# Turning q, k and y by one transposing DMA per block instead of on TensorE, in a gated linear attention and feed-forward kernel

## The chip, the cores and the metric

The kernel runs on one core of a Trainium2 chip. The metric is the device time of one execution in microseconds. Engines are named as in the profile: PE is TensorE's matrix multiply, PEld its weight loads, DVE is VectorE, ACT is ScalarE, POOL is GpSimd, and SP is SyncE, which here does nothing but issue DMAs. "SPq" and "ACTq" are DMAs issued by SP and by ACT.

## The reference

A gated linear attention over 4 batches, 8 heads, 768 steps and a head size of 48 is followed by a feed-forward layer with 384 inputs, 2048 hidden units, and the activation s * relu(h)^2 + b.

```
for t in range(S):
    state = alpha[:, :, t, :, None] * state + np.einsum('bhd,bhe->bhde', k[:, :, t], v[:, :, t])
    y[:, :, t] = np.einsum('bhd,bhde->bhe', q[:, :, t], state)
x = y.transpose(0, 2, 1, 3).reshape(B * S, H * D)
h = x @ w_in
r = np.maximum(h, 0.0)
g = s * (r * r) + b
out = g @ w_out
```

Inputs and output are float32; the kernel multiplies in bfloat16.

## The kernel before

The 3072 rows are worked through in 24 blocks of 128 steps, six to a batch. In one block the attention is computed in its chunked form, with all 8 heads beside each other (48 columns each, in pairs of heads):

- `ln` takes the logarithm of alpha on ACT, `cum` sums it over the block by a matmul with a triangular matrix, and ACT gives the cumulative decay `b_sb` and its inverse `bi_sb`. `decay` brings the block's last row of `b_sb` to the layout of `blast`: one DMA to DRAM (`row_dr`) and two back from there, all issued by SP.
- `qk` scales q and k on DVE (`qb_sb`, `kb_sb`, with time on the partitions). `vcast` casts v on POOL.
- `tr` turns scaled q and k on PE, eight transposes by an identity (L244) into `ct_ps`, and DVE copies them to `qkT_sb` (L249), with the head's columns on the partitions.
- `amat` multiplies k by q per head into `a_ps` and masks the result on DVE.
- `y` (that is, `yp` and `st`) gives the block's output in `y_ps` from `am` and v and from the state `sd_sb` of the block before, and the new state by PE, DVE (`t1_sb`) and POOL (`sd_sb`, `sc_sb`). ACT copies `y_ps` to `y_bf` (L305).
- `xt` turns `y_bf` on PE by three transposes into `h_ps` (L312), and ACT copies them to `xd_sb` (L318), the input of the feed-forward layer.
- `m`, four times a block (u = 0 to 3), multiplies `xd_sb` by a quarter of w_in (twelve matmuls, L365), takes relu on ACT (`r_sb`, L379) and squares it on DVE (`gt_sb`, L386). This is what "products" means in this document. `o`, four times a block, multiplies `gt_sb` by a quarter of w_out (L402). After the fourth, blocks 0 to 12 are kept in SBUF by an ACT copy (`keep_sb`, in the space of the w_in staging), since the bias row isn't known yet; the later ones get the bias added on DVE (L415) and go out through `store` (L438). The kept blocks get theirs by `add_bias` (L441), one every 5.5 positions from position 117.3 on, each with a `store` of its own.

Inputs are loaded per block by four DMAs on SP (`load`: alpha, k, q, v, 192 KB each, in rows of 192 bytes), five blocks ahead, into rings of eight buffers. Other rings have two or three buffers. Two PSUM banks `h_ps` serve the products in turn, with `xt` between them.

Each engine runs its instructions in the order in which the program issues them. That order is written out by hand: `at(position, function, ...)` puts a piece of work at a position, and at the end all pieces are called in order of position. Block n has its `y` at p = 8n, so eight positions are one block. For a block in the steady part, `cum` stands at p - 14.8, `qk` right behind, `tr` at p - 10.8, `amat` at p - 7.9, `y` at p, `xt` at p + 1, `m` at p + 2.5 to p + 7.5, `o` at p + 8.5 to p + 14.5. SP's queue is ordered by the same positions: what stands in it behind a waiting DMA waits too. A DMA's completion is counted on one of eight semaphores, which are used in turn.

Of the kernel before, what the change touches and what calls it, by code (L numbers as in the profile page):

```python
# [9 lines left out]
BF16 = mybir.dt.bfloat16  # L10
# [4 lines left out]
def kernel(  # L15
# [12 lines left out]
    nc = tc.nc  # L28
# [34 lines left out]
    def ring(name, shape, dtype, n):  # L63
        return [sb.tile(shape, dtype, name=f"{name}{i}") for i in range(n)]
# [33 lines left out]
    for g, sz in enumerate(GROUPS):  # L98
        first_block.append(sum(GROUPS[:g]))
        u0 = first_block[g] % UNITS  # L100
        xd_sb.append(xd_all[:, u0 : u0 + sz].rearrange("a u x -> a (u x)").rearrange("a (t s) -> a t s", t=KT))
# [106 lines left out]
    def cum(n):  # L208
        la = la_sb[n % 2]
        nc.tensor.matmul(out=cum_ps, lhsT=U_bf, rhs=la[:, :, 0:48], start=True, stop=True)  # L210
# [12 lines left out]
        if n < NCH - 1:  # L223
            nc.scalar.activation(out=blast[n % 3][0:112, :, 0], in_=tot_ps[0:112], func=AF.Exp)
        elif n % NCH < NCH - 1:
            decay(n)

    def decay(n):
        row = row_dr[n % 3]
        nc.sync.dma_start(out=row, in_=b_sb[n % 2].rearrange("s h d -> s (h d)")[127:128])  # L230
        for e in range(2):
            nc.sync.dma_start(
                out=blast[n % 3][64 * e : 64 * e + 48, :, 0],
                in_=row.rearrange("o (p e d) -> e d (o p)", e=2, d=48)[e],
            )

    def qk(n):
        nc.vector.tensor_tensor(out=kb_sb[n % 3][:, :, 0:48], in0=k_sb[n % NLD], in1=bi_sb[n % 2], op=ALU.mult)  # L238
        nc.vector.tensor_tensor(out=qb_sb[n % 2][:, :, 0:48], in0=q_sb[n % NLD], in1=b_sb[n % 2], op=ALU.mult)  # L239

    def tr(n):
        for x, t in ((0, qb_sb[n % 2]), (1, kb_sb[n % 3])):
            for p in range(NP):
                nc.tensor.transpose(  # L244
                    out=t_ps[0:112, x, p, :],
                    in_=t.rearrange("a h d -> a (h d)")[:, 128 * p : 128 * p + 112],
                    identity=ident,
                )
        nc.vector.tensor_copy(  # L249
            out=qkT_sb[n % 2][0:112].rearrange("a x p t -> a (x p t)"),  # L250
            in_=t_ps[0:112].rearrange("a x p t -> a (x p t)"),
        )

    def amat(n):
        qkT = qkT_sb[n % 2]
        for p in range(NP):
            for e in range(2):
                r0 = 64 * e
                nc.tensor.matmul(  # L259
                    out=a_ps[e][:, p, :],  # L260
                    lhsT=qkT[r0 : r0 + 48, 1, p, :],
                    rhs=qkT[r0 : r0 + 48, 0, p, :],
                    start=True,
                    stop=True,
                )
        for e in range(2):
            nc.vector.tensor_tensor(out=am_sb[e][n % 2], in0=a_ps[e], in1=mask4, op=ALU.mult)  # L267
# [6 lines left out]
    def yp(n):  # L274
        c = n % NCH
        if c > 0:
            for p in range(NP):
                nc.tensor.matmul(  # L278
                    out=y_ps[:, 96 * p : 96 * p + 96],
                    lhsT=qkT_sb[n % 2][0:112, 0, p, :],  # L280
                    rhs=sd_sb[(n - 1) % 2][0:112, p, :],
                    start=(p == 0),
                    stop=False,
                    skip_group_check=True,
                )
        for h in range(H):
            nc.tensor.matmul(  # L287
                out=y_ps[:, 48 * h : 48 * h + 48],
                lhsT=am_sb[h % 2][n % 2][:, h // 2, :],
                rhs=v_bf[n % 3][:, h, :],  # L290
                start=(c == 0 and h == 0),
                stop=(h == H - 1),
                skip_group_check=True,
            )
        if c < NCH - 1:
            kb = kb_sb[n % 3].rearrange("a h d -> a (h d)")
            for p in range(NP):
                nc.tensor.matmul(
                    out=pst[:, p, :],
                    lhsT=kb[:, 128 * p : 128 * p + 128],  # L300
                    rhs=v_bf[n % 3][:, 2 * p : 2 * p + 2, :],
                    start=True,
                    stop=True,
                )
        nc.scalar.activation(out=y_bf[n % 2], in_=y_ps[:, 0 : H * 48], func=AF.Copy)  # L305


    def xt(n):
        hp = h_ps[nrelu[0] % 2].bitcast(BF16)[:, 0 : KT * C]
        nrelu[0] += 1  # L310
        for kk in range(KT):
            nc.tensor.transpose(  # L312
                out=hp[:, kk * C : (kk + 1) * C],
                in_=y_bf[n % 2][:, 128 * kk : 128 * (kk + 1)],
                identity=ident,
            )
        g, i = group_of[n]
        nc.scalar.activation(  # L318
            out=xd_sb[g][:, :, i * C : (i + 1) * C],
            in_=hp.rearrange("a (t s) -> a t s", t=KT),  # L320
            func=AF.Copy,
        )
# [71 lines left out]
    def mm2(g, t, u):  # L394
        if g == NBLK - 1:
            return last(u)
        N = GROUPS[g] * C
        op = o_ps
        if g in o_in_a:
            op = a_ps[o_in_a[g]].rearrange("a p t -> a (p t)")  # L400
        for j in range(4 * u, 4 * u + 4):
            nc.tensor.matmul(  # L402
                out=op[:, 0:d_model],
                lhsT=gt_sb[g][:, j * N + t * C : j * N + (t + 1) * C],
                rhs=w_out_bf[:, j, :],
                start=(j == 0),
                stop=(j == NJ - 1),
            )
        if u == 3:
            if g < NKEEP:  # L410
                nc.scalar.activation(out=keep_sb[g], in_=op[:, 0:d_model], func=AF.Copy)
                return
            ot = out_sb[nout[0] % 3]
            nout[0] += 1
            nc.vector.tensor_tensor(out=ot, in0=op[:, 0:d_model], in1=bias_w, op=ALU.add)  # L415
            store(g, ot)


    def last(u):
# [43 lines left out]
    for t in la_sb:  # L463
        nc.vector.memset(t, 0.0)
    nc.vector.memset(ones_c, 1.0)
    for t in qb_sb + kb_sb + blast:
        nc.vector.memset(t, 0.0)
    make_identity(nc, ident)
    for i in range(NP):
# [64 lines left out]
        at(111.5 + 2 * i, bias_row, i)  # L534
    for n in range(NKEEP):
        at(117.3 + 5.5 * n, add_bias, n)
        at(118.2 + 5.5 * n, store, n, keep_sb[n])
    for u in range(1, 4):
        at((30.5, 31.2, 32.5)[u - 1], o, 3, u)
    at(20.0, load, NLD)  # L540
    for n in range(4, NBLK):
        p = 8 * n
        if n > 4:
# [8 lines left out]
        at(p, y, n)  # L552
        if n + 5 < NBLK:
# [37 lines left out]
```

## Time and profile before

| | before |
|---|---|
| median of 3 runs | 199.65 us (199.53 to 199.88) |
| the profiled execution's span, from the first to the last instruction | 198.2 us |
| PE busy | 185.2 us (93%) |
| DVE busy | 150.8 us (76%) |
| ACT busy | 118.8 us (60%) |
| POOL busy | 64.2 us (32%) |
| moved by DMA | 30.33 MB, 113454 packets |

Durations in this document come from one profiled execution. Its span is 1.45 us shorter than the median of the runs; what lies between is before the first instruction and after the last. In the chain of waits each piece is put down to the instruction that ended last; a group of pipelined matmuls counts there with what it adds, which is less than the sum of its instructions' durations.

### The profile page before, as it was taken

Reading aid. Unit: us, or ns where it says so; the run is one execution under the profiler, and the core shown is the slowest. Engines: PE = TensorE matmul, PEld = TensorE weight load, DVE = VectorE, ACT = ScalarE, POOL = GpSimd, SP = SyncE. Lnnn points to the kernel's source line nnn. Section 1 sums busy time; section 2 is a strip of 40 time slices with the busy share of each in tenths; the row PEclk is TensorE's granted clock in tenths of the full one; section 3 lists DMA queues with packets and bytes.
Section 4 is the critical chain, followed back from the end, with each engine's and each line's share of the span. In section 5 each row is a group of like instructions: output and inputs, shape, how many; then the busy total and the mean of one; then the engine's idle time right before and its main releaser. Section 6 shows DMA issues by size and latency. Waiting matters only on the chain.

```text
span 198.2 us, 6120 instructions
## 1 busy us (share of the span) xinstructions
PE 185.2 (93%) x2440; PEld 145.3 (73%) x2440; DVE 150.8 (76%) x296; ACT 118.8 (60%) x243; POOL 64.2 (32%) x96
## 2 busy tenths in 40 slices
PE   1999899988899999999999999999999999999994
PEld 1566587754577688888878877878888877877783
DVE  5467777867466779789877996989987999998532
ACT  3245668381675765766766677666575665664650
POOL 5142251611120136326500633623700851652000
PEclk9999999999999999999999999999999999999999
DMA  7999999999999384693968846958947953122212
GB/s 125 189 342 232 314 283 369 199 177 193 187 172 195 60 142 86 101 159 64 195 84 148 134 68 120 159 93 193 229 87 164 161 176 112 41 82 81 87 37 79
DMA packets 113454, 30.33 MB, mean 153 GB/s; under 512 B 106627, under 2 KB 111890, under 8 KB 113426
## 3 DMA queue, kind: packets, MB, share of 16 engines
q1 hardware_dynamic: 109262, 29.15, 73.7%
q10 hardware_dynamic: 4164, 0.79, 2.8%
q8 instruction: 19, 0.31, 0.7%
q14 instruction: 9, 0.07, 0.1%
HBM read 25.19 MB, written 4.74 MB: 151 GB/s over the span
## 4 chain that ended last, share of the span: by engine, by line
PE 68%; SPq 15%; DMA 10%; DVE 3%; ACT 1%; issue 1%; ACTq 0%; DVEq 0%
PE h_ps L365 25%; PE o_ps L402 25%; DMA q_sb<-in_q_dram 8%; SPq L128 5%; PE ct_ps L244 5%; SPq L147 4%; PE a_ps L259 3%; SPq L125 3%; SPq L122 2%; PE ct_ps L210 2%; PE y_ps L287 2%; PE h_ps L312 2%; DMA al_sb<-in_alpha_dram 2%; SPq L131 1%; PE a_ps L425 1%; PE y_ps L278 1%
## 5 line engine op out<-in xcount | busy, mean ns | idle before, releaser
L379 ACT ACTIVATE r_sb<-h_ps 128x512 bf16<-128x512 f32 x94 | 55.8, 597 | 39.2 <-PE h_ps L365 37.6
L365 PE MATMUL h_ps<-xd_all,w_in_bf 128*128 128x128 bf16 x1128 | 74.8, 219 | 1.5 <-ACT r_sb L379 1.1
L365 PEld LDWEIGHTS <-w_in_bf 128*128 128x128 bf16 x1152 | 69.3, 98 | 8.4 <-issue 2.3
L402 PE MATMUL o_ps<-w_out_bf,gt_all 128*128 128x384 bf16 x336 | 68.5, 326 | 1.4 <-DVE w_out_bf L160 0.7
L386 DVE TENSOR_TENSOR gt_all<-r_sb 128x512 bf16<-128x512 bf16 x96 | 45.3, 484 | 26.5 <-ACT r_sb L379 25.8
L339 POOL TENSOR_TENSOR sd_sb<-t_sb,blast 48x192 bf16<-48x192 f32 x40 | 22.5, 563 | 103.5 <-DVE t_sb L334 67.3
L402 PEld LDWEIGHTS <-gt_all 128*128 128x128 bf16 x368 | 32.5, 98 | 17.4 <-issue 1.8
L343 POOL TENSOR_TENSOR sc_sb<-t_sb,blast 112x384 f32<-112x384 f32 x16 | 21.8, 1362 | 1.3
L206 POOL CAST v_bf<-v_sb 128x384 bf16<-128x384 f32 x24 | 17.7, 744 | 12.9 <-DMA v_sb<-in_v_dram 12.7
L318 ACT ACTIVATE xd_all<-h_ps 128x384 bf16<-128x384 bf16 x24 | 11.8, 490 | 15.5 <-PE h_ps L312 15.5
L249 DVE COPY qkT<-ct_ps 112x1024 bf16<-112x1024 bf16 x24 | 16.4, 685 | 4.8 <-PE ct_ps L244 4.7
L238 DVE TENSOR_TENSOR kb_sb<-k_sb,bi_sb 128x384 bf16<-128x384 f32 x24 | 13.7, 569 | 8.3 <-ACT bi_sb L221 8.2
L267 DVE TENSOR_TENSOR am_a<-a_ps,mask 128x512 bf16<-128x512 f32 x24 | 16.4, 683 | 3.1 <-PE a_ps L259 3.1
L239 DVE TENSOR_TENSOR qb_sb<-q_sb,b_sb 128x384 bf16<-128x384 f32 x24 | 16.7, 694 | 0.0
L267 DVE TENSOR_TENSOR am_b<-a_ps,mask 128x512 bf16<-128x512 f32 x24 | 16.3, 681 | 0.0
L221 ACT ACTIVATE bi_sb<-ct_ps 128x384 f32<-128x384 f32 x24 | 11.7, 487 | 5.2 <-PE ct_ps L213 3.9
L305 ACT ACTIVATE y_bf<-y_ps 128x384 bf16<-128x384 f32 x24 | 11.7, 488 | 4.9 <-PE y_ps L287 4.8
L203 ACT ACTIVATE la_sb<-al_sb 128x384 bf16<-128x384 f32 x24 | 12.4, 516 | 3.6 <-DMA al_sb<-in_alpha_dram 3.6
L210 PE MATMUL ct_ps<-la_sb,U_bf 128*128 128x384 bf16 x24 | 8.2, 340 | 4.6 <-ACT la_sb L203 4.6
L222 ACT ACTIVATE b_sb<-ct_ps 128x384 f32<-128x384 f32 x24 | 11.9, 494 | 0.0
L244 PEld LDWEIGHTS <-qb_sb 128*112 128x112 bf16 x96 | 8.5, 136 | 4.4 <-DVE qb_sb L239 3.2
L259 PE MATMUL a_ps<-qkT 48*128 48x128 bf16 x192 | 10.2, 226 | 1.0 <-DVE qkT L249 0.4
(66 smaller groups left out, 195.0 us busy)
## 6 DMA issues: line engine op xcount, KB each, us to landing
al_sb<-in_alpha_dram SPq DMA_DIRECT2D x24, 192.0 KB, 3.2
k_sb<-in_k_dram SPq DMA_DIRECT2D x24, 192.0 KB, 3.6
q_sb<-in_q_dram SPq DMA_DIRECT2D x22, 192.0 KB, 4.7
v_sb<-in_v_dram SPq DMA_DIRECT2D x22, 192.0 KB, 4.9
w_in_st<-in_moe_w_in_dram SPq DMA_DIRECT2D x4, 768.0 KB
w_out_st<-in_moe_w_out_dram SPq DMA_DIRECT2D x4, 768.0 KB
out_dram<-w_in_st SPq DMA_DIRECT2D x13, 192.0 KB, 2.6
out_dram<-out_sb SPq DMA_DIRECT2D x10, 192.0 KB, 3.4
```

What stands on the lines that cost most here:

```text
L206: nc.gpsimd.tensor_copy(out=v_bf[n % 3], in_=v_sb[n % NLD])
L239: nc.vector.tensor_tensor(out=qb_sb[n % 2][:, :, 0:48], in0=q_sb[n % NLD], in1=b_sb[n % 2], op=ALU.mult)
L244: nc.tensor.transpose(out=t_ps[0:112, x, p, :], in_=t.rearrange("a h d -> a (h d)")[:, 128 * p : 128 * p + 112], identity=ident,)
L249: nc.vector.tensor_copy(out=qkT_sb[n % 2][0:112].rearrange("a x p t -> a (x p t)"), in_=t_ps[0:112].rearrange("a x p t -> a (x p t)"),)
L259: nc.tensor.matmul(out=a_ps[e][:, p, :], lhsT=qkT[r0 : r0 + 48, 1, p, :], rhs=qkT[r0 : r0 + 48, 0, p, :], start=True, stop=True,)
L267: nc.vector.tensor_tensor(out=am_sb[e][n % 2], in0=a_ps[e], in1=mask4, op=ALU.mult)
L339: nc.gpsimd.tensor_tensor(out=sd[r, :, d], in0=t1_sb[r, :, d], in1=bl[r].to_broadcast([48, NP, 48]), op=ALU.mult)
L343: nc.gpsimd.tensor_tensor(out=sc_sb[0:112], in0=t1_sb[0:112], in1=bl[0:112].to_broadcast([112, NP, 96]), op=ALU.mult)
L365: nc.tensor.matmul(out=hp[:, jj * N : (jj + 1) * N], lhsT=w_in_bf[:, kk, 128 * j : 128 * (j + 1)], rhs=xd_sb[g][:, kk, 0:N], start=(kk == ...
L379: nc.scalar.activation(out=rs, in_=h_of.pop((g, u)), func=AF.Relu)
L386: nc.vector.tensor_tensor(out=gt_sb[g][:, u * 512 : (u + 1) * 512], in0=rs, in1=rs, op=ALU.mult)
L402: nc.tensor.matmul(out=op[:, 0:d_model], lhsT=gt_sb[g][:, j * N + t * C : j * N + (t + 1) * C], rhs=w_out_bf[:, j, :], start=(j == 0), sto ...
```

## The change

From block 6 on (`TURN = 6`), up to block 21, `xt` is no longer called, and from block 8 on `tr` neither. In their place `turn(n)` issues one transposing DMA on SP. Its source is a new tile of 128 x 1408 bfloat16 with scaled q and k of block n + 2 (1024 columns) and y of block n (384 columns) side by side; its destination is a tile of 128 x 11 x 128 that holds the eight turned squares of q and k and the three of y. The places that read `qkT_sb` and `xd_sb` read views of it. Both tiles are rings of three.

```diff
+    TURN = 6
-    qb_sb = ring("qb_sb", [128, H, 64], BF16, 2)
-    kb_sb = ring("kb_sb", [128, H, 64], BF16, 3)
+    QK = 2 * H * 64
+    rows_sb = ring("rows_sb", [128, QK + H * 48], BF16, 3)
+    qk_sb = [t[:, 0:QK] for t in rows_sb]
...
-    y_bf = ring("y_bf", [128, H * 48], BF16, 2)
-    qkT_sb = ring("qkT", [128, 2, NP, 128], BF16, 2)
+    cols_sb = ring("cols_sb", [128, 2 * NP + KT, 128], BF16, 3)
+    qkT_sb = [t[:, 0 : 2 * NP].rearrange("a (x p) t -> a x p t", x=2) for t in cols_sb]
...
+        if TURN <= g < NBLK - 2:
+            xd_sb.append(cols_sb[(g + 2) % 3][:, 2 * NP :])
...
+    def turn(n):
+        nc.sync.dma_start_transpose(out=cols_sb[(n + 2) % 3], in_=rows_sb[(n + 2) % 3])
...
-        nc.scalar.activation(out=y_bf[n % 2], in_=y_ps[:, 0 : H * 48], func=AF.Copy)
+        nc.scalar.activation(out=rows_sb[(n + 2) % 3][:, QK:], in_=y_ps[:, 0 : H * 48], func=AF.Copy)
```

For q and k of block n + 2 to be there in time, `ln`, `vcast`, `cum` and `qk` move to p - 19 from block 8 on, and `amat` to p - 6. The row of `decay` is sent to DRAM in `cum`, and its two DMAs back stand six positions later. `turn(n)` stands at p + 0.5 and the loads behind it at p + 0.6. Products and outputs stand up to five positions later (two for block 6, three for 7, four for 8, five from block 9, and less again in the last two blocks).

```diff
         elif n % NCH < NCH - 1:
-            decay(n)
+            nc.sync.dma_start(out=row_dr[n % 3], in_=b_sb[n % 2].rearrange("s h d -> s (h d)")[127:128])
...
+            if n >= TURN + 2:
+                c = 19.0
...
-            at(p - t, tr, n)
-            at(p - a, amat, n)
+            if n < TURN + 2:
+                at(p - t, tr, n)
+                at(p - a, amat, n)
+                at(p - c + 0.3, decay, n)
+            else:
+                at(p - 6.0, amat, n)
+                at(p - 13.0, decay, n)
         at(p, y, n)
+        if turned:
+            at(p + 0.5, turn, n)
+        else:
+            at(p + 1.0, xt, n)
         if n + 5 < NBLK:
-            at(p - 4.0, load, n + NLD - 3)
+            at(p + 0.6 if turned else p - 4.0, load, n + NLD - 3)
+        late = min(max(n - 4, 0), 5.0) if n < NBLK - 2 else (NBLK - 1 - n) * 3.5
         for u in range(4):
-            at(p + (2.5, 3.5, 5.5, 7.5)[u], m, n, u)
-            at(p + (8.5, 9.5, 12.5, 14.5)[u], o, n, u)
-        at(p + 1.0, xt, n)
+            at(p + late + (2.5, 3.5, 5.5, 7.5)[u], m, n, u)
+            at(p + late + (8.5, 9.5, 12.5, 14.5)[u], o, n, u)
+        if NKEEP <= n < NBLK - 1:
+            at(p + late + 16.2, store, n)
```

All stores but the last block's are issued by ACT instead of SP: those of the kept blocks two positions behind their `add_bias` (before 0.9), those of the later blocks 1.7 positions behind their last `o` (before at once).

```diff
-    def store(n, o):
-        nc.sync.dma_start(out=out[n * C : (n + 1) * C, :], in_=o)
+    finished = {n: keep_sb[n] for n in range(NKEEP)}
+
+    def store(n):
+        nc.scalar.dma_start(out=out[n * C : (n + 1) * C, :], in_=finished.pop(n))
```

More of the change, by code (lines that the diff above doesn't have):

```diff
@@ L81 @@
     bi_sb = ring("bi_sb", [128, H, 48], FP32, 2)
-    qb_sb = ring("qb_sb", [128, H, 64], BF16, 2)
-    kb_sb = ring("kb_sb", [128, H, 64], BF16, 3)
+    QK = 2 * H * 64
+    rows_sb = ring("rows_sb", [128, QK + H * 48], BF16, 3)
+    qk_sb = [t[:, 0:QK] for t in rows_sb]
+    qb_sb = [t.rearrange("a (x h d) -> a x h d", x=2, h=H)[:, 0] for t in qk_sb]
+    kb_sb = [t.rearrange("a (x h d) -> a x h d", x=2, h=H)[:, 1] for t in qk_sb]
     v_bf = ring("v_bf", [128, H, 48], BF16, 3)
-    y_bf = ring("y_bf", [128, H * 48], BF16, 2)
-    qkT_sb = ring("qkT", [128, 2, NP, 128], BF16, 2)
+    cols_sb = ring("cols_sb", [128, 2 * NP + KT, 128], BF16, 3)
+    qkT_sb = [t[:, 0 : 2 * NP].rearrange("a (x p) t -> a x p t", x=2) for t in cols_sb]
     am_sb = [ring("am_a", [128, NP, 128], BF16, 2), ring("am_b", [128, NP, 128], BF16, 2)]
@@ L100 @@
         u0 = first_block[g] % UNITS
-        xd_sb.append(xd_all[:, u0 : u0 + sz].rearrange("a u x -> a (u x)").rearrange("a (t s) -> a t s", t=KT))
+        if TURN <= g < NBLK - 2:
+            xd_sb.append(cols_sb[(g + 2) % 3][:, 2 * NP :])
+        else:
+            xd_sb.append(xd_all[:, u0 : u0 + sz].rearrange("a u x -> a (u x)").rearrange("a (t s) -> a t s", t=KT))
         gt_sb.append(gt_all[:, u0 : u0 + sz].rearrange("a u x -> a (u x)"))
@@ L225, in cum @@
         elif n % NCH < NCH - 1:
-            decay(n)
+            nc.sync.dma_start(out=row_dr[n % 3], in_=b_sb[n % 2].rearrange("s h d -> s (h d)")[127:128])
     def decay(n):
         row = row_dr[n % 3]
-        nc.sync.dma_start(out=row, in_=b_sb[n % 2].rearrange("s h d -> s (h d)")[127:128])
+        if n < NCH - 1 or n % NCH == NCH - 1:
+            return
         for e in range(2):
@@ L238, in qk @@
         nc.vector.tensor_tensor(out=kb_sb[n % 3][:, :, 0:48], in0=k_sb[n % NLD], in1=bi_sb[n % 2], op=ALU.mult)
-        nc.vector.tensor_tensor(out=qb_sb[n % 2][:, :, 0:48], in0=q_sb[n % NLD], in1=b_sb[n % 2], op=ALU.mult)
+        nc.vector.tensor_tensor(out=qb_sb[n % 3][:, :, 0:48], in0=q_sb[n % NLD], in1=b_sb[n % 2], op=ALU.mult)
+    def turn(n):
+        nc.sync.dma_start_transpose(out=cols_sb[(n + 2) % 3], in_=rows_sb[(n + 2) % 3])
     def tr(n):
-        for x, t in ((0, qb_sb[n % 2]), (1, kb_sb[n % 3])):
+        for x, t in ((0, qb_sb[n % 3]), (1, kb_sb[n % 3])):
             for p in range(NP):
@@ L249, in tr @@
         nc.vector.tensor_copy(
-            out=qkT_sb[n % 2][0:112].rearrange("a x p t -> a (x p t)"),
+            out=qkT_sb[n % 3][0:112].rearrange("a x p t -> a (x p t)"),
             in_=t_ps[0:112].rearrange("a x p t -> a (x p t)"),
@@ L254, in amat @@
     def amat(n):
-        qkT = qkT_sb[n % 2]
+        qkT = qkT_sb[n % 3]
         for p in range(NP):
@@ L279, in yp @@
                     out=y_ps[:, 96 * p : 96 * p + 96],
-                    lhsT=qkT_sb[n % 2][0:112, 0, p, :],
+                    lhsT=qkT_sb[n % 3][0:112, 0, p, :],
                     rhs=sd_sb[(n - 1) % 2][0:112, p, :],
@@ L313, in xt @@
                 out=hp[:, kk * C : (kk + 1) * C],
[L314 removed]
+                in_=rows_sb[(n + 2) % 3][:, QK:][:, 128 * kk : 128 * (kk + 1)],
                 identity=ident,
@@ L415, in mm2 @@
             nc.vector.tensor_tensor(out=ot, in0=op[:, 0:d_model], in1=bias_w, op=ALU.add)
-            store(g, ot)
+            finished[g] = ot
     def last(u):
@@ L465 @@
     nc.vector.memset(ones_c, 1.0)
-    for t in qb_sb + kb_sb + blast:
+    for t in qk_sb + blast:
         nc.vector.memset(t, 0.0)
@@ L536 @@
         at(117.3 + 5.5 * n, add_bias, n)
-        at(118.2 + 5.5 * n, store, n, keep_sb[n])
+        at(119.3 + 5.5 * n, store, n)
     for u in range(1, 4):
@@ L542 @@
         p = 8 * n
+        turned = TURN <= n < NBLK - 2
         if n > 4:
@@ L549 @@
             at(p - c + 0.2, qk, n)
-            at(p - t, tr, n)
-            at(p - a, amat, n)
+            if n < TURN + 2:
[5 more added lines that the diff above has]
+                at(p - 13.0, decay, n)
         at(p, y, n)
+        if turned:
+            at(p + 0.5, turn, n)
+        else:
+            at(p + 1.0, xt, n)
         if n + 5 < NBLK:
-            at(p - 4.0, load, n + NLD - 3)
+            at(p + 0.6 if turned else p - 4.0, load, n + NLD - 3)
+        late = min(max(n - 4, 0), 5.0) if n < NBLK - 2 else (NBLK - 1 - n) * 3.5
         for u in range(4):
-            at(p + (2.5, 3.5, 5.5, 7.5)[u], m, n, u)
-            at(p + (8.5, 9.5, 12.5, 14.5)[u], o, n, u)
-        at(p + 1.0, xt, n)
+            at(p + late + (2.5, 3.5, 5.5, 7.5)[u], m, n, u)
+            at(p + late + (8.5, 9.5, 12.5, 14.5)[u], o, n, u)
+        if NKEEP <= n < NBLK - 1:
+            at(p + late + 16.2, store, n)
     for _, _, fn, args in sorted(events, key=lambda e: e[:2]):
```

## The prediction

> **What bounds the kernel now.** I read the busy time by stage first, then the chain of waits inside one stage, then the groups of the instructions that the change removes, then the DMA issues and SP's queue. All times are from one profiled execution with a span of 198.2 us; the median of the runs is 199.65 us, so 1.45 us lie outside the span, and I add them at the end. Three stages of one block each, from the view of busy time by window (PE, PEld, DVE, ACT and POOL busy, TensorE clock, DMA share, GB/s):
>
> ```profile
> 74.38:81.42 7.04, 7.04 (x101) 5.79 (x102) 5.53 (x11) 4.81 (x11) 3.23 (x4) 1.00 0.74 121
> 81.42:88.46 7.04, 7.04 (x101) 5.79 (x102) 6.24 (x12) 4.81 (x11) 3.22 (x4) 1.00 0.71 114
> ```
>
> PE is busy all of the 7.04 us of a block, at the full clock; DVE has 0.8 us left, ACT 2.2 us. The chain of waits through the next block (start, length, what) confirms it: every piece is PE.
>
> ```profile
> 88.46 0.76 PE o_ps L402 x4
> 89.21 0.17 PE h_ps L312 x3
> 89.38 0.16 PE ct_ps L210
> ...
> 91.53 0.65 PE o_ps L402 x4
> 92.18 0.45 PE ct_ps L244 x8
> 92.63 0.67 PE h_ps L365 x12
> ...
> 95.17 0.33 PE a_ps L259 x8
> ```
>
> Here a group costs what it adds to the chain, not the duration of its instructions: eight transposes of q and k 0.45 us, three of y 0.17 us, a group of twelve h_ps matmuls 0.67, four o_ps matmuls 0.65. From block 6 (66 us) to the end the kernel is this chain, so PE time saved there is time saved. Before 58 us the chain runs through loads and nothing of the change acts there.
>
> ```profile
> L318 ACT ACTIVATE xd_all<-h_ps 128x384 bf16<-128x384 bf16 x24 | 11.8, 490 | 15.5 <-PE h_ps L312 15.5
> L249 DVE COPY qkT<-ct_ps 112x1024 bf16<-112x1024 bf16 x24 | 16.4, 685 | 4.8 <-PE ct_ps L244 4.7
> ```
>
> These two copies (0.49 us ACT, 0.69 us DVE per block) go with the transposes; both engines have room, so they are worth nothing by themselves. The DMA issues (KB, us from issue to landing) and SP's queue in one block:
>
> ```profile
> al_sb<-in_alpha_dram SPq DMA_DIRECT2D x24, 192.0 KB, 3.2
> ...
> v_sb<-in_v_dram SPq DMA_DIRECT2D x22, 192.0 KB, 4.9
> ...
> blast<-row_dr SPq DMA_DIRECT2D x30, 0.8 KB, 1.9
> ```
>
> ```profile
> 82.62 0.90 SPq L232 DMA_DIRECT2D blast<-row_dr  x2
> 83.58 0.44 SPq L122 DMA_DIRECT2D al_sb<-in_alpha_dram  x1
> 84.11 0.53 SPq L128 DMA_DIRECT2D k_sb<-in_k_dram  x1
> 84.73 0.81 SPq L125 DMA_DIRECT2D q_sb<-in_q_dram  x1
> 85.60 0.72 SPq L131 DMA_DIRECT2D v_sb<-in_v_dram  x1
> 86.42 0.58 SPq L230 DMA_DIRECT2D row_dr<-b_sb  x1
> 89.59 1.81 SPq L232 DMA_DIRECT2D blast<-row_dr  x2
> ```
>
> SP issues for about 4.1 us a block (0.90 + 0.44 + 0.53 + 0.81 + 0.72 + 0.58, and gaps), and stands still from 87.0 to 89.6 because L232 waits for the row of L230. The DMA engines are taken for 0.55 to 0.74 of a block.
>
> **The change part by part.** *Removed from PE:* for 16 blocks (8 to 23) the q and k transposes, 16 x 0.45 = 7.2 us; for 16 blocks (6 to 21) those of y, 16 x 0.17 = 2.7 us. Both lie on the chain: -9.9 us. A block falls from 7.04 to 6.42 us.
>
> *Added: 16 transposing DMAs on SP.* Each moves 128 x 1408 x 2 bytes = 352 KB as 1408 rows of 256 bytes. The trace holds no such DMA. Its landing time, l, is bounded below by the smallest DMA (1.9 us), and by the nearest rows of size it lies between 1.9 + (3.2 - 1.9) x 1408/1024 = 3.7 (by pieces; a load is 128 x 8 = 1024 pieces) and 1.9 + 1.3 x 352/192 = 4.3 (by bytes). The v load, which queues behind three others on the same queue, takes 4.9. The upper end is open: if it ran element by element, 180,224 elements at the 21 ns per packet and engine that the queue's row gives (73.7% of 16 x 198.2 us over 109,262 packets), over 16 engines, it would be some 240 us. I take 3.7, since the loads are bound by pieces (192 bytes each).
>
> *What l may be.* In the changed program's order, PE has between the end of y(n) and the first product of block n three product groups, four output groups, one amat and one cum: 3 x 0.67 + 4 x 0.65 + 0.33 + 0.17 = 5.1 us. Against it stand the copy of y on ACT (0.13 us until it starts, 0.49 long) and l. So l up to 5.1 - 0.6 = 4.5 us is wholly hidden by these products, which is what the shift by five positions buys. At l = 3.7 the cover has 0.8 us to spare. The shift is not yet whole for blocks 6, 7 and 8 (2, 3 and 4 positions of 0.8 us instead of 5), so they have 2.4, 1.6 and 0.8 us less: stalls of 1.6, 0.8 and 0 us. That is +2.4 us. For q and k of block n + 2 the same DMA has ten positions, 8 us: hidden.
>
> *SP.* The transposing DMA waits for y on ACT and q, k on DVE; behind it stand the four loads of block n + 5 (five blocks, some 30 us, ahead of need), then the two decay DMAs of block n + 2, needed ten positions later by POOL. The row's DMA moves ahead by six positions, so the 2.6 us stand at L232 go. SP's sum is 4.1 us plus the new issue, between 0.25 us (a row's) and 1.85 us (the longest store issue): at most 6.0 of 6.42 us. Cost nothing; that cover is the empty 2.3 us.
>
> *DMA engines.* Loads hold them at most 0.74 x 7.04 = 5.2 us a block, and in stages full of loads (8 to 32 us) the share reads 1.2, so packets overlap; the new 1408 pieces add 1408/1024 of one load, that is 0.34 of a block's four: in all 7.0 us of share, at 1.2 a real 5.8 us of 6.42. Cost nothing, with little room.
>
> *Stores on ACT.* 23 store issues move from SP to ACT, one or two a block from block 15. The shortest issue on either queue is 0.33 to 0.41 us. ACT falls to 4.81 - 0.49 = 4.3 us a block and so has 2.1 us; two stores take 0.8. What stands behind a store is the next relu, for which PE waits after two groups (1.3 us). The store also waits for DVE's sum and, because completion counters are shared in turn, for an earlier DMA. Bounds: 0 and 23 x 0.43 = 9.9 us (each issue in full). I take +0.5 us, nearer to hidden.
>
> *Earlier cum, qk.* Four positions earlier from block 8, five blocks of loads ahead: nothing.
>
> **Sum:** 198.2 - 9.9 + 2.4 + 0.5 = 191.2 us of span, and 1.45 outside: **192.6 us**, 3.5% less.
>
> **Rivals.** *A, the loop over the transposing DMA (slower).* y(n), its copy, the DMA and the first product of n now stand in one ring with y(n + 1): the block takes l + 0.6 + 0.67 + 0.64 (product group, y) = l + 1.9 us as soon as that is above 6.42. It breaks even at l = 5.1 and loses beyond. For it speaks the v load's 4.9 us on the same queue, and that loads still in flight from the block before would stand ahead of the transposing DMA; against it that they then have a block's length to drain. At l = 5.6 a block takes 7.5: 16 x 0.5 = 8 us more than before, 208 us.
>
> *B, SP or its queue sets the pace while loads run (blocks 6 to 18, 13 blocks).* If the issue or the transfer takes 1 us more than I take, a block there stays at 6.7 to 7.0, and 13 x 0.3 to 13 x 0.6 = 4 to 8 us of the gain go: 196.5 to 200.5 us, 198 in the middle. DMA share 0.74 speaks for it, the removed stand at L232 against.
>
> *C, a much longer transfer.* If small pieces made it 10 us, a block would take 11.9, 16 x 4.9 = 78 us more: 278 us. No row shows a DMA that rearranges, so the trace can't exclude it; the 192-byte pieces of the loads move at 114 to 121 GB/s beside all else, which speaks against. The Trainium skill (VectorE: DVE Perf Modes, The three transpose paths) speaks for it: it gives 1309 ns for a 128x128 block by this path, against 390 by TensorE; eleven blocks in a row would be an estimated 14.4 us and the kernel some 350 us. In the Trainium skill's Advanced Engine Details and Errata, X-Bar Transpose (TRN2), such DMAs are as fast as plain ones; by that the sum stands. No run so far shows which holds.
>
> *D, ACT's stores take the gain back.* The upper bound of 9.9 us cancels the saving: 199 to 202 us.
>
> **Chances.** Forecast 0.48 (its own range 190 to 195); A 0.25; B 0.15; C 0.07; D 0.05. About 0.2% (0.4 us) is what a measurement of this kernel can tell from no change. Faster: 0.48 and 0.12 of B, 0.60. Within 0.2%: 0.01 of B, 0.02 of D, 0.03. Slower: A, C, the rest of B and D, 0.37. The range runs from 190, where no early stall remains, through B and most of A, to 209; C and the far part of A are left out.
>
> **What would show it.** Right: in blocks 9 to 20 a block of 6.4 us with PE busy throughout, L244 gone after block 7, the new DMA landing in under 4.5 us, PE waiting for it only in blocks 6 to 8, and no relu late behind a store. A shows as PE idle ahead of the first h_ps group, released by a DMA on cols, in each block; B as the same, but gone when the loads end; D as PE waiting for r_sb with ACT's queue held at the store. I am wrong altogether if l is not between 1.9 and 5.

## The result, and the profile after

The changed kernel takes 215.97 us (median of 4 runs, 214.18 to 217.51) against 199.59 us: 1.0776 times as long, interval 1.0706 to 1.0847. The ratio is taken over the fast runs of both kernels, here without the one of 217.51 us, so it isn't the quotient of the two medians. The kernel is slower by 15.5 us (0.0776 x 199.6), where 192.6 us was forecast, and it lies 7 us above the upper end of the range.

| | before | after |
|---|---|---|
| span of the profiled execution | 198.2 us | 212.4 us |
| PE busy | 185.2 us (93%) | 178.3 us (84%) |
| DVE busy | 150.8 us (76%) | 138.2 us (65%) |
| ACT busy | 118.8 us (60%) | 111.5 us (52%) |
| PE idle, from 40 us to its last instruction | 2.9 us | 22.0 us |
| `y` of block 6, `y` of block 23, end | 66.3, 186.6, 198.2 us | 67.5, 197.4, 212.4 us |

PE has less to do, as meant, but 19.0 us more of idle time. The loss is spread: 1.2 us ahead of block 6, 9.6 us between blocks 6 and 23, and 3.4 us in the tail.

The busy time by window, for single blocks from `y` to `y` (PE, PEld, DVE, ACT and POOL busy, TensorE clock, DMA share, GB/s), after the change:

```profile
113.75:120.49 6.74, 6.74 (x93) 5.03 (x90) 4.95 (x10) 4.26 (x9) 2.55 (x4) 1.00 1.06 170
166.59:175.09 8.50, 6.75 (x94) 5.02 (x92) 5.32 (x11) 3.95 (x8) 2.54 (x4) 1.00 0.97 186
```

The matmuls on PE fall from 101 to 93 or 94 in a block, and PE's busy time from 7.04 to 6.75 us. But blocks without a gap, like that at 113.75, are rare; that at 166.59 lasts 8.50 us. The DMA share is about 1, where it was 0.71 to 0.74. The groups of the two copies confirm that the work is gone (8 left of 24 each):

```profile
L260 DVE COPY cols_sb<-ct_ps 112x1024 bf16<-112x1024 bf16 x8 | 5.5, 689 | 4.6 <-PE ct_ps L255 4.6
L329 ACT ACTIVATE xd_all<-h_ps 128x384 bf16<-128x384 bf16 x8 | 3.9, 488 | 2.5 <-PE h_ps L323 2.5
```

What PE waits for, from the view of waits (total, times, longest):

```profile
PE h_ps L376 <- DMA cols_sb<-rows_sb: 9.7, 7, 4.0
PE o_ps L413 <- DVE out_sb L426: 6.0, 9, 1.7
```

Neither wait was among PE's waits before. The first is the new DMA: products wait for y. The second has nothing to do with a transposition: the outputs of the next block wait for DVE to read the sum of the last one out of the bank `o_ps`. The DMA issues (landing in the last column):

```profile
v_sb<-in_v_dram SPq DMA_DIRECT2D x22, 192.0 KB, 4.8
...
blast<-row_dr SPq DMA_DIRECT2D x30, 0.8 KB, 3.1
...
cols_sb<-rows_sb SPq DMA_TRANSPOSE x16, 4.1
```

The transposing DMA lands in 4.1 us (3.6 to 4.4, in the seven of sixteen cases in which the trace tells the landing), within the 4.5 us that the forecast allowed it. SP's queue through one block, after the change (start, length, what):

```profile
108.77 1.39 SPq L250 DMA_TRANSPOSE cols_sb<-rows_sb  x1
110.20 1.02 SPq L129 DMA_DIRECT2D al_sb<-in_alpha_dram  x1
111.27 0.62 SPq L135 DMA_DIRECT2D k_sb<-in_k_dram  x1
111.94 1.06 SPq L132 DMA_DIRECT2D q_sb<-in_q_dram  x1
113.05 1.01 SPq L138 DMA_DIRECT2D v_sb<-in_v_dram  x1
114.16 1.38 SPq L240 DMA_DIRECT2D blast<-row_dr  x2
...
115.99 1.39 SPq L250 DMA_TRANSPOSE cols_sb<-rows_sb  x1
```

SP issues without a break from one transposing DMA to the next, 7.2 us. ACT had y for the second one ready at 114.92, and the DMA was issued 1.07 us later, because SP was still issuing the loads and the decay.

The chain of waits at block 6, where the longest stall is:

```profile
69.72 0.06 SPq L233
...
69.93 4.44 DMA cols_sb<-rows_sb
...
74.41 1.46 PE h_ps L376 x12
75.87 0.32 PE ct_ps L217
76.19 1.22 PE o_ps L413 x4
```

The DMA was issued 1.58 us after ACT's copy of y (which ended at 68.35), behind the row DMAs of two blocks on SP, and PE stood still from 70.40 to 74.41. Then twelve products take 1.46 us and four outputs 1.22, where they otherwise take 0.67 and 0.65; the row of the window from 73.80 to 77.21 us, which begins in the last 0.6 us of the stall, gives a granted clock of 0.50:

```profile
73.80:77.21 3.41, 2.80 (x17) 2.01 (x18) 0.67 (x2) 1.30 (x3) 0.00 (x0) 0.50 1.17 194
```

Finally the chain late in the kernel, after the change:

```profile
176.39 0.61 ACT r_sb L390
...
177.02 0.54 DVE gt_all L397
177.56 0.78 DVE w_in_st L454
178.34 0.47 DVE am_a L278
...
178.87 0.68 DVE am_b L278
179.54 0.33 DVE gt_all L397
179.87 0.48 DVE out_sb L426
...
180.40 1.46 PE o_ps L413 x8
```

For four microseconds no step of the chain is PE. DVE squares, adds the bias of a kept block (`w_in_st`), masks both halves of `amat`, squares again, and only then sums the output of the finished block, for which `o_ps` waits. PE has other work for most of this time and stands idle for the last 0.86 us. In the kernel before, the same sum stood ahead of the masks. DVE's timeline there, where the next block's `y` starts at 151.7 us (start, length, what, idle time before it):

```profile
151.30 0.43 DVE L386 TENSOR_TENSOR gt_all<-r_sb 128x512 bf16<-128x512 bf16 x1 [0.61 <-ACT r_sb L379]
151.65 0.55 DVE L415 TENSOR_TENSOR out_sb<-o_ps,bias_w 128x384 f32<-128x384 f32 x1
...
153.43 0.68 DVE L267 TENSOR_TENSOR am_a<-a_ps,mask 128x512 bf16<-128x512 f32 x1
```

So there are two candidates: the DMA with its queue, and the new order of the work, which the forecast had costed at nothing.

### The profile page after: what moved, and what is told of

The parts are those of the page before. It is cut to its first block, busy times and chain, and to the rows that moved or that the text cites. A ratio compares the mean times of both kernels' runs of the same rounds, so it can differ in the third digit from the quotient of the medians.

```text
span 212.4 us, 5725 instructions
## 1 busy us (share of the span) xinstructions
PE 178.3 (84%) x2264; PEld 133.3 (63%) x2264; DVE 138.2 (65%) x278; ACT 111.5 (52%) x227; POOL 54.2 (25%) x96
## 4 chain that ended last, share of the span: by engine, by line
PE 40%; DMA 18%; DVE 12%; ACT 7%; issue 4%; SPq 1%; ACTq 0%
PE h_ps L376 16%; PE o_ps L413 14%; DMA cols_sb<-rows_sb 13%; ACT r_sb L390 5%; DMA row_dr<-b_sb 3%; DVE gt_all L397 3%; PE y_ps L298 2%; DVE out_sb L426 2%; DMA k_sb<-in_k_dram 2%; DVE w_in_st L454 2%; PE a_ps L270 1%; DVE am_a L278 1%; DVE am_b L278 1%; PE a_ps L436 1%; PE p_ps L309 1%
## 5 line engine op out<-in xcount | busy, mean ns | idle before, releaser
L376 PE MATMUL h_ps<-cols_sb,w_in_bf 128*128 128x128 bf16 x768 | 53.9, 221 | 9.7 <-DMA cols_sb<-rows_sb 9.7
L376 PE MATMUL h_ps<-xd_all,w_in_bf 128*128 128x128 bf16 x360 | 23.9, 219 | 2.0 <-ACT r_sb L390 1.4
L213 POOL CAST v_bf<-v_sb 128x384 bf16<-128x384 f32 x24 | 14.0, 587 | 22.8 <-DMA v_sb<-in_v_dram 12.1
L246 DVE TENSOR_TENSOR rows_sb<-k_sb,bi_sb 128x384 bf16<-128x384 f32 x24 | 13.7, 569 | 8.1 <-ACT bi_sb L228 8.1
L228 ACT ACTIVATE bi_sb<-ct_ps 128x384 f32<-128x384 f32 x24 | 11.7, 488 | 7.9 <-PE ct_ps L220 3.6
L354 POOL TENSOR_TENSOR sc_sb<-t_sb,blast 112x384 f32<-112x384 f32 x16 | 14.0, 874 | 1.3
L247 DVE TENSOR_TENSOR rows_sb<-q_sb,b_sb 128x384 bf16<-128x384 f32 x24 | 13.5, 564 | 1.1 <-ACT b_sb L229 1.1
L316 ACT ACTIVATE rows_sb<-y_ps 128x384 bf16<-128x384 f32 x24 | 11.7, 486 | 4.6 <-PE y_ps L298 3.3
L270 PE MATMUL a_ps<-cols_sb 48*128 48x128 bf16 x192 | 9.8, 220 | 1.2 <-DVE cols_sb L260 0.4
L270 PEld LDWEIGHTS <-cols_sb 48*128 48x128 bf16 x192 | 5.6, 95 | 8.4 <-issue 4.7
L298 PE MATMUL y_ps<-v_bf,am_b 128*128 128x48 bf16 x96 | 8.1, 184 | 1.0 <-DVE am_b L278 1.0
```

The lines of the kernel that those rows point to most:

```text
L213: nc.gpsimd.tensor_copy(out=v_bf[n % 3], in_=v_sb[n % NLD])
L247: nc.vector.tensor_tensor(out=qb_sb[n % 3][:, :, 0:48], in0=q_sb[n % NLD], in1=b_sb[n % 2], op=ALU.mult)
L270: nc.tensor.matmul(out=a_ps[e][:, p, :], lhsT=qkT[r0 : r0 + 48, 1, p, :], rhs=qkT[r0 : r0 + 48, 0, p, :], start=True, stop=True,)
L298: nc.tensor.matmul(out=y_ps[:, 48 * h : 48 * h + 48], lhsT=am_sb[h % 2][n % 2][:, h // 2, :], rhs=v_bf[n % 3][:, h, :], start=(c == 0 and ...
L354: nc.gpsimd.tensor_tensor(out=sc_sb[0:112], in0=t1_sb[0:112], in1=bl[0:112].to_broadcast([112, NP, 96]), op=ALU.mult)
L376: nc.tensor.matmul(out=hp[:, jj * N : (jj + 1) * N], lhsT=w_in_bf[:, kk, 128 * j : 128 * (j + 1)], rhs=xd_sb[g][:, kk, 0:N], start=(kk == ...
```

## The experiments

Losses below are the ratio less one, times 199.6 us, so that runs beside different runs of the kernel before can be added.

### Is it the DMA or the order?

`e1_order_only` keeps the whole order, the buffers and the stores of the changed kernel, and turns q, k and y on PE again, so that no transposing DMA is left.

```diff
+                at(p - 15.0, tr, n)
...
-        if turned:
-            at(p + 0.5, turn, n)
-        else:
-            at(p + 1.0, xt, n)
+        at(p + 1.0, xt, n)
```

> The changed kernel's order, buffers and stores on ACT, but q, k and y are turned on PE as before (q and k 15 positions ahead of their y, y one position behind it), with no transposing DMA. Theory 1 (the loop from y over the transposing DMA to the products costs the time): the order by itself is harmless, 199 to 203 us, at most the 3.4 us of a longer end more than before. Theory 2 (the new order costs it: products five positions later put o's bank turnaround next to amat's masks on DVE, 6 us of waits for L426, and a longer end): 207 us or more, with PE's waits for the output's sum on DVE still there.

Measured: ratio 1.0688 (1.0626 to 1.075), +13.7 us. Without any transposing DMA nearly the whole loss is there. `o_ps` waits for `out_sb` 4.4 us in 9 waits. The difference from the changed kernel, 1.8 us, lies within the two intervals, which overlap: what the DMA saves on PE, it costs again. In this same order PE is busy 190.0 us with the transposes and 178.3 us without.

`e3_idle_turn` is the other half: the kernel before, with a transposing DMA of the same size between two tiles that nobody reads, one a block.

```diff
+    def turn(n):
+        nc.sync.dma_start_transpose(out=spare_out[n % 3], in_=spare_in)
...
+        if 6 <= n < NBLK - 2:
+            at(p + 0.5, turn, n)
```

> The kernel before, with a transposing DMA of the full size (352 KB) added per block from 6 to 21, at the changed kernel's place, from a constant tile to a tile that nobody reads. Theory 1: the DMA by itself costs nothing, 199.5 to 200.5 us. Theory 4 (contention on SP's queue and the DMA engines): 203 us or more.

Measured: ratio 1.0969 (1.0878 to 1.106), +19.3 us, for a DMA that nobody waits for. Two lines of its view of waits, and the chain at one of the places:

```profile
ACT b_sb L224 <- DMA row_dr<-b_sb: 18.1, 8, 4.4
...
PE ct_ps L249 <- DVE qb_sb L241: 12.1, 7, 3.7
```

```profile
174.99 2.34 DMA row_dr<-b_sb
...
177.41 0.50 ACT b_sb L224
...
178.55 0.65 PE ct_ps L249 x8
```

In the order of before, the small row DMA comes onto SP's queue behind the transposing one, and SP falls behind. It issued this row, of block 19, 18.1 us after ACT had it ready (before 1.8 us), and from block 8 on all rows were issued 8 to 18 us late (before at most 6.7). From the issue to the start of the reads that wait for the row it is 1.8 to 3.5 us, hardly more than the 1.2 to 3.3 us before: what is late is SP, not the row's transfer. ACT can't overwrite `b_sb` until the row has been read, and `qb_sb` and the transposes wait for that. Part of the loss is the clock, which was 0.50 in three stretches of 13.7 us in all; half of the 12.6 us for which PE was busy in them, an estimated 6 us, is lost that way. So a transposing DMA needs another place in the order; the two halves can't simply be added.

`e4_stores_act` is the kernel before with the stores on ACT alone.

```diff
-        nc.sync.dma_start(out=out[n * C : (n + 1) * C, :], in_=o)
+        nc.scalar.dma_start(out=out[n * C : (n + 1) * C, :], in_=finished.pop(n))
...
+            at(p + 16.2, store, n)
```

> The kernel before, with the stores issued by ACT at the changed kernel's distances behind their sums, nothing else. Theory 1: 199.5 to 200.5 us. Theory 3 (stores in ACT's queue hold up the relus): 202 us or more, with ACT's relus waiting for DMAs on the output.

Measured: ratio 1.0042 (1.0004 to 1.008), +0.8 us, near the forecast's 0.5. It is not the stores.

### Which part of the order?

`e6_products_late` is the kernel before with the shift of products and outputs alone:

```diff
+        late = min(max(n - 4, 0), 5.0) if n < NBLK - 2 else (NBLK - 1 - n) * 3.5
...
+            at(p + late + (2.5, 3.5, 5.5, 7.5)[u], m, n, u)
+            at(p + late + (8.5, 9.5, 12.5, 14.5)[u], o, n, u)
```

> The kernel before, with products and outputs up to five positions later, as in the changed kernel, and nothing else changed (turned on PE, stores on SP). Theory 2 (the shift of products and outputs against amat and y is what the order costs): 208 us or more, with o_ps waiting for the output's sum on DVE, blocks of 7.4 us and more. If the cost in e1 is in the earlier cum and the later amat, or in the stores: 203 us or less.

Measured: ratio 1.0431 (1.0407 to 1.0456), +8.6 us. Its chain in the block at 138 us shows the pattern of the changed kernel, without anything else of the change:

```profile
138.43 0.61 ACT r_sb L379
...
139.40 0.55 DVE t_sb L334
139.95 0.60 DVE am_a L267
...
141.06 0.45 DVE w_in_st L441
...
141.95 0.47 DVE kb_sb L238
142.41 0.47 DVE qb_sb L239
...
143.22 0.48 DVE out_sb L415
...
143.74 1.46 PE o_ps L402 x8
```

Five positions of eight put the fourth output of a block, and with it DVE's sum, in the middle of a block (position 3.5 of eight) instead of near its end (6.5). There DVE has the state, the masks and the scaling of q and k ahead of it, all issued earlier; and the next output needs the one bank `o_ps`. Blocks 15 to 21 take 7.3 to 8.5 us, where before they took 6.9 to 7.1. The idle time with a name explains only part (8.3 us of idle time against 2.9); the rest lies in groups on PE that take longer next to each other, and I have not attributed it.

`e8_cum_early` is the kernel before with the other shift alone: `cum` and `qk` at p - 19, `tr` at p - 15, `amat` at p - 6.

```diff
+            if n >= 8:
+                c, t, a = 19.0, 15.0, 6.0
```

> The kernel before, with cum, qk (19 positions ahead of y), tr (15) and amat (6) of blocks 8 and later where the order of e1 has them; products, outputs, decay and stores stand where they were. Theory 2 as above (products' shift): 203 us or less. If the earlier cum and later amat are the cost: 208 us or more.

Measured: ratio 1.0326 (1.0277 to 1.0374), +6.5 us. Block 5, in which the first moved `cum` falls, takes 9.48 us instead of 8.08; the chain there:

```profile
64.07 3.08 DMA row_dr<-b_sb
...
67.23 0.50 ACT b_sb L222
...
67.78 0.61 PE ct_ps L244 x8
```

`cum` of block 8 lands shortly before `tr` of block 7 and uses the same bank `ct_ps`; its second half, `b_sb`, must wait until the row of block 6 has been read out of one of only two buffers, and the row's DMA stands behind four loads. The changed kernel has the same piece (3.23 us from 63.16). Its blocks 15 to 21 take 7.0 to 7.6 us (before 6.9 to 7.1), with waits for `out_sb`. The time, 206.57 us, fell between the two expectations. The three parts give 8.6 + 6.5 + 0.8 = 15.9 us, against 13.7 (12.5 to 15.0) together in `e1_order_only`. So the parts account for the order's loss and somewhat more. The places of the loads and of the decay and the rings of three, which `e1_order_only` also has, were not run alone.

`e13_late8_on_pe` asks whether it is the delay or its phase: as `e6_products_late`, but up to eight positions, a whole block, so that the output's sum comes back to where it stood within a block.

```diff
+        late = {20: 6.5, 21: 5.0, 22: 3.5, 23: 0.0}.get(n, min(max(n - 4, 0), 8.0))
```

> As e6_products_late (everything on PE, only products and outputs later), with up to eight positions, a whole block, instead of five. If it is the place of products and outputs within the block that costs (after five positions the output's sum stands on DVE behind amat's masks, the state, a square and the scaling, while the next output group waits for the one o bank; after eight it stands where it was), the blocks from 12 to 19 take 7.1 us and the whole 201 to 205 us. If the depth itself costs: 208 us or more.

Measured: ratio 1.0352 (1.0282 to 1.0422), +7.0 us; the expectation of 201 to 205 us was missed. But the two halves of the answer are in the windows, of a block with the whole delay and of one where it is taken back:

```profile
150.86:157.96 7.10, 7.10 (x104) 5.71 (x102) 6.47 (x14) 4.44 (x9) 4.03 (x4) 1.00 0.66 135
172.09:182.48 10.39, 9.37 (x125) 7.16 (x123) 7.62 (x15) 4.98 (x10) 2.47 (x4) 1.00 0.21 77
```

With eight positions the steady blocks (15 to 20) run at 6.9 to 7.1 us without a wait: it is the phase that costs there. The rest is lost in the ramps. Eight positions hold back one block of products and outputs, 4 x (0.67 + 0.65) = 5.3 us; `y` of block 21 starts only 0.9 us earlier than before (172.1 against 173.0), so about 4.4 us were lost up to there; from there to the end it takes 9.0 us more than before, 3.7 more than the work held back.

`e7_late8` tried the same delay on the changed kernel, where it would give the DMA more cover too.

```diff
-        late = min(max(n - 4, 0), 5.0) if n < NBLK - 2 else (NBLK - 1 - n) * 3.5
+        late = {20: 6.5, 21: 5.0, 22: 3.5, 23: 0.0}.get(n, min(max(n - 4, 0), 8.0))
```

> The changed kernel with products and outputs up to eight positions later instead of five, a whole block, so that they stand to y and o to its bank as they did before the change, and the transposing DMA has 2.4 us more of cover. Theory 1 and 2 together: no wait of h_ps for cols from block 12 on and less for the output's sum, 203 to 210 us. If it is neither the landing time nor the place of the outputs: 214 us or more.

Measured: ratio 1.0897 (1.0859 to 1.0935), 218.4 us, worse than the change and far from the 203 to 210 us expected. The waits of products over the DMA fall to 6.1 us, but `a_ps` now waits for it 4.2 us, and the blocks of the ramp back take 11.7 and 9.4 us. I missed this by not costing the ramp.

### What does waiting for the DMA cost?

`e11_stale_y` is the changed kernel whose products read the y of the block before.

```diff
-            xd_sb.append(cols_sb[(g + 2) % 3][:, 2 * NP :])
+            xd_sb.append(cols_sb[(g + 1 + (g == TURN)) % 3][:, 2 * NP :])
```

> The changed kernel, but the products of blocks 7 to 21 read the y of the block before (the part of the transposing DMA before), so that they never wait for their own; all work, DMAs and the order are the same, and the output is not the reference's. Theory 1 + 2 (order 15 us, the wait over the DMA takes back the 9.9 us that PE saves): the waits of h_ps for cols go but for block 6, 9 us less, 204 to 208 us, and the rest above 189 is the order's. If the order alone explains it and the DMA's time is harmless: 214 us or more.

Measured: ratio 1.0575 (1.0543 to 1.0607), 4.0 us less than the changed kernel (0.0201 x 199.6). From its view of waits:

```profile
PE o_ps L413 <- DVE out_sb L426: 6.2, 9, 1.7
...
PE h_ps L376 <- DMA cols_sb<-rows_sb: 3.9, 1, 3.9
...
PE a_ps L270 <- DMA cols_sb<-rows_sb: 2.5, 4, 1.0
```

The waits of the later blocks are gone (block 6 still waits for its own DMA), new ones of 2.5 us have come for q and k, and the waits for `out_sb` are untouched. So the loop over y, with its DMA, is worth some 4 us of the 15.5; 11.5 us would stay if y came at once from block 7 on. The 4 us may be too few: behind the wait of block 6 the clock was 0.50 for 6.83 us here, and for 3.41 us in the changed kernel. I had expected 204 to 208 us and got 211.65: most of the loss is elsewhere, in the order.

### Can q and k alone gain?

Scaled q and k are ready a block ahead, so they can bear the DMA's length without any shift of the products. `e2_qk_only` turns these two alone by DMA (256 KB), y on PE, products, outputs and stores as before.

```diff
-        nc.sync.dma_start_transpose(out=cols_sb[(n + 2) % 3], in_=rows_sb[(n + 2) % 3])
+        nc.sync.dma_start_transpose(out=cols_sb[n % 3], in_=rows_sb[n % 3])
...
+                at(p - 16.0, turn, n)
...
+        at(p + 1.0, xt, n)
```

> The kernel before, with q and k of blocks 8 to 23 turned by one transposing DMA of 256 KB per block, issued 16 positions ahead of their y, so that no y waits for it; y is turned on PE, products, outputs and stores stand where they were. Theory 1 (the loop over y): no loop, so 16 x 0.45 = 7.2 us fall away and nothing replaces them, 192 to 194 us. Theory 4 (SP's queue and the DMA engines can't carry the transposing DMAs beside the loads): 198 us or more, with PE waiting for these or for the loads.

Measured: ratio 1.0463 (1.0386 to 1.0541), in the range of theory 4. Undisturbed blocks take 6.68 us, but `a_ps` waits for the DMA 10.1 us in 8 waits: SP stands at the decay's reads behind the row 14.2 us in 11 waits, and the next transposing DMA stands behind it. `e5_qk_reordered` puts the loads right behind the transposing DMA, the decay's reads later, and brings the first blocks' `cum` forward step by step.

```diff
-                c = 19.0
+                c, a = {8: (16.0, 4.5), 9: (18.0, 7.0)}.get(n, (19.0, 7.9))
...
-                at(p - 13.0, decay, n)
+                at(p - c + 7.0, decay, n)
...
-            at(p - 4.0, load, n + NLD - 3)
+            at(p + 0.6 if n >= TURN else p - 4.0, load, n + NLD - 3)
```

> As e2_qk_only (q and k by DMA, y on PE, products and outputs where they were), but SP's queue is put in another order: the four loads stand right behind the transposing DMA and the decay's reads four positions behind that, so that SP doesn't stand still for the row; and the first two turned blocks get their cum only one and three positions earlier, so that it doesn't meet the transposes of block 7 in the same PSUM bank. Theory 1b (in e2 it was SP's queue, which took 8 us a block with its stand of 2.7 us for the row, that made the transposing DMA late): 192 to 195 us, blocks of 6.6 us, no wait of a_ps for cols. Theory 4 (the DMA engines can't carry it): 200 us or more, with a landing of 5 us and more.

Measured: ratio 1.0175 (1.0129 to 1.022). Most blocks now take 6.6 to 6.8 us; four wait for the DMA (1.73, 1.17, 2.13 and 1.69 us), three of them from 152 us on, where SP issues loads, two stores a block and the transposing DMA almost without a pause. Neither theory fits: the time lies in the range of theory 4, but where the trace tells the DMA's landing it is 3.0 us, not 5. My next expectation put the waits down to stores that wait for DVE's sums, but from 145 to 173 us SP stands at a store for at most 0.6 us at a time. `e9_qk_act` moves the stores to ACT and the loads a little back; `e10_qk_sp_late` is the same with the late positions of the stores but on SP.

```diff
-        nc.sync.dma_start(out=out[n * C : (n + 1) * C, :], in_=o)
+        nc.scalar.dma_start(out=out[n * C : (n + 1) * C, :], in_=finished.pop(n))
```

> As e5_qk_reordered, with the stores on ACT at the changed kernel's distances and the loads 1.2 positions behind y instead of 0.6, so that no transposing DMA stands behind a store or behind loads that it needn't follow. Theory 1b (in e5 SP's queue, held by stores that wait for DVE's sums, made the transposing DMAs of the last blocks late: 1.2, 2.1 and 1.7 us of waits, and 1.7 us once behind loads): these waits go, 195 to 198.5 us, under the kernel before. Theory 4 (the DMA engines): the waits stay, 202 us or more.

> As e9_qk_act, but the stores stay on SP, only at the later positions, where their sums are done when SP comes to them. If it is the stand of SP at a store that counts, and not the store's issue: as e9, 195 to 199 us. If SP has no time for the issues beside the transposing DMA: 201 us or more.

Measured: 1.0072 (1.0037 to 1.0107) on ACT and 1.0069 (1.0032 to 1.0105) on SP: each a little slower than before, and both expectations of less than before were missed. On ACT, one wait for the DMA is left (1.2 us), and blocks with stores lose by an ACT that is late instead; on SP, what is left is two waits at blocks 19 and 20, where loads, two stores a block and the transposing DMA come together. `e12_stores_spread` changes one thing more, the kept blocks' stores, which go out later and closer together once the loads have ended.

```diff
-        at(119.3 + 5.5 * n, store, n)
+        at(max(119.3 + 5.5 * n, 147.0 + 3.2 * n), store, n)
```

> As e10_qk_sp_late (q and k by DMA, y on PE, stores on SP), but the stores of the kept blocks are spread over positions 147 to 185, one every 3.2 positions, so that they stand mostly behind the last load (position 146) instead of among the loads from 119 on. If SP's own time is what made the last transposing DMAs late (in e10 SP issues for 9 us a block there, and PE waits 1.8 and 2.4 us): these waits go, 195.5 to 199 us. If not, 201 us or more.

Measured: 198.36 us, ratio 0.9876 (0.982 to 0.9933): faster than before, by 2.5 us (1.3 to 3.6). Two of its blocks, with the loads and with the stores:

```profile
88.02:94.70 6.68, 6.68 (x96) 5.31 (x94) 5.17 (x11) 4.76 (x10) 2.28 (x4) 1.00 1.11 167
149.65:156.33 6.68, 6.68 (x96) 5.31 (x93) 5.46 (x13) 4.31 (x9) 2.75 (x4) 1.00 0.86 157
```

PE is busy throughout, with 96 instructions instead of 101 to 105, and a block takes 6.68 us instead of 7.04. So the saving of 0.36 us a block for q and k is real, if the chain of waits stays PE's. Over 16 blocks that would be 5.8 us; PE's idle time from 40 us on is 2.0 us longer than before (5.0 against 2.9), and one wait over the DMA is left in it, 1.0 us in the block at 73 us.

## Why the prediction was wrong, step by step

- **PE is the bound, and the transposes lie on its chain (-9.9 us): right in kind.** Blocks without a wait show it: 6.68 us for q and k alone (0.36 saved, 0.45 forecast), 6.74 in the changed kernel at 113.75 us, where 6.42 was forecast. For q and k the saving was four fifths of the term. What the transposes of y saved by themselves no run shows: the block of 6.74 us has lost both kinds and is 0.30 us shorter.
- **"Earlier cum, qk. Four positions earlier from block 8 ...: nothing." This step failed, and with it the shift by five positions, which the forecast counted as cover only.** The runs gave +6.5 us for the one, +8.6 us for the other and +13.7 us together with the moved stores. The forecast asked whether the inputs come in time. It did not ask what each moved group stands behind on DVE, nor who waits for a PSUM bank or a buffer that is now released later.
- **DVE's 0.8 us of room** was read as enough for work that gets less. It was less in sum (138.2 us instead of 150.8), but its order decided: in the chain from 176.39 us on, 0.6 us of ACT and 3.3 us of DVE stood ahead of the next block's first output.
- **l = 3.7 us: nearly right (4.1).** Rival C is out. The two pages of the Trainium skill that the forecast set against each other are told apart by this: eleven squares land in 4.1 us, not in the 14.4 us estimated as eleven times the 1309 ns for one square in the Trainium skill's VectorE: DVE Perf Modes (The three transpose paths). The trace agrees with the Trainium skill's Advanced Engine Details and Errata (X-Bar Transpose (TRN2)), by which such a DMA is as fast as a plain one: a load of v, 192 KB from DRAM and behind three others, lands in 4.8 us here. The forecast's sign of being wrong altogether, an l outside 1.9 to 5, did not show: it was wrong with an l inside.
- **Early stalls, +2.4 us: too small.** Blocks 6 to 8 stood 4.0, 1.6 and 0.8 us, 6.4 in all. At block 6 the forecast had 1.6; SP's queue added 1.6 and the landing 0.7 (4.4 instead of 3.7). Then the clock: the groups behind that gap took 0.79 + 0.16 + 0.57 = 1.5 us more than usual (1.46, 0.32 and 1.22 against 0.67, 0.16 and 0.65).
- **SP cost nothing (at most 6.0 of 6.42 us): wrong, rival B's mechanism.** The new issue, 1.39 us in the middle of 16, lay within its bounds (the longest took 2.93), but the four loads' issues grew from 2.5 us in the block that the forecast read to 3.7 in the one shown above (by medians from 70 to 150 us, from 2.5 to 3.1), and SP was full for 7.2 us of that block. In nine of sixteen blocks the DMA went out at once behind the copy of y; in the other seven 0.9 to 2.4 us later. With the whole shift there were four waits, 3.2 us together, and three of them (1.04, 0.47 and 1.37 us) behind such a late issue.
- **The sum.** The 9.9 us forecast as saved met 9.7 us of waits for the DMA, so that nothing was left of them: the changed kernel and `e1_order_only` differ by 1.8 us, within the intervals. The slow clock isn't the DMA's alone, since `e1_order_only` has such a stretch as well (0.50 from 68.55 to 71.96 us). The order's 13.7 us stand alone.
- **Rival A** (every block waits for the loop over the DMA) did not happen as drawn: 7 of 16 blocks waited. **Rival D** is out with +0.8 us in the order of before; in the changed kernel ACT's relus stood behind a store twice (2.8 and 1.9 us), but PE waited for `r_sb` only before 31 us.

Still open: about a third of the order's loss (in `e1_order_only` 15.6 us of span, but 10.5 us more of idle time on PE) lies in groups on PE that take longer, without a wait that the trace names. Half of the 3.41 us at a clock of 0.50, an estimated 1.7 us, is one part of that; the rest is not attributed. And I did not find an order that brings y, too, through the DMA at a gain.

## What to carry to other kernels

A shift in an order written by hand is not free because its inputs are early: write down, for each engine, what the moved work stands behind, and who waits for the buffer or bank that it now releases later, and price the ramps into and out of the shift. Move to a DMA what is known long ahead (q and k here) before what is on the loop (y), and treat the issuing engine's queue as a full resource, since a DMA that is short on its own is late when four others stand ahead of it. An engine's sum of busy time says nothing on whether it delivers the one result that the bound engine needs next.

## What the runs showed of the hardware

- In the changed kernel PE stood still from 70.40 to 74.41 us; the granted clock was 0.50 from 73.80 to 77.21, and groups took about twice as long for some 3 us. Behind stalls of 2.6 us (`e1_order_only`, 0.50 from 68.55 to 71.96) and 2.2 us (`e3_idle_turn`, 0.50 from 150.92 to 154.33) it fell too; behind one of 1.6 us in the changed kernel it stayed at 1.00 (window from 82 to 86 us). A stall can cost more than its own length.
- A transposing DMA of 128 x 1408 bfloat16 between two SBUF tiles held SP for 1.3 to 2.9 us (1.4 in the middle) in the changed kernel and landed in 3.6 to 4.4 us; in the other runs that have it, it landed in 3.5 to 6.2 us. One of 128 x 1024 landed in 3.1 to 3.7 us in `e12_stores_spread`, and in 3.0 to 5.2 us over all runs that have it.
- In `e3_idle_turn` a row of 1.5 KB behind it on SP's queue was issued so late, up to 18.1 us after it was ready, that ACT waited up to 4.4 us for it (18.1 us in 8 waits). The kernel before has no wait of ACT for it. Once issued, the row was there about as soon as before.
